# Query and key projections split at group ends, last output tile in halves, written orders replaced

## The chip, the cores and the metric

The kernel runs on one core of a Trainium2 chip. The metric is the device time of one execution in microseconds (us). Five engines work side by side: TensorE (PE in the profile; PEld is its weight load), VectorE (DVE), ScalarE (ACT), GpSimd (POOL) and SyncE (SP), whose queue issues nearly all DMAs here. Each takes its instructions in the order in which the program has them, and waits at an instruction until the semaphores it names have been raised.

## The reference

Two layers follow each other. The first is attention within chunks of 64 tokens, for 8 batches and 8 heads of 64 columns; its output, the heads side by side, is `x` (576 tokens by 512 columns per batch). The second sends `x` through four experts with causal attention over all 576 tokens, and adds the two best experts of each token with softmax weights:

```python
scores = scale * np.matmul(q_c, k_c.transpose(0, 1, 2, 4, 3))      # chunks of 64
attn = softmax(scores); out = np.matmul(attn, v_c)                 # -> x
logits = x @ w_gate; topk = argpartition(-logits, 2); w = softmax(selected logits)
for e in range(E):
    q = x @ wq[e]; k = x @ wk[e]; v = x @ wv[e]
    a = softmax(causal(scale * (q @ k.transpose(0, 2, 1))))
    ye = a @ v @ wo[e]
    out += (weight of e, where e is among the two best) * ye
```

## The kernel before

**Tiles and stages.** The 8 batches of 576 tokens are 36 groups of 128 tokens, nine to every two batches, so a batch is four and a half groups. In an even batch the groups start at columns 0, 128, 256, 384 and 512, and the last one is shared with the next batch; in an odd batch the shared half fills columns 0 to 64 and groups start at 64, 192, 320 and 448. The first five groups are worked one by one, the others mostly in pairs (`UNITS`).

`stage_a` does the first layer of a unit: scores on PE (L471, small 64x64 matmuls on quarters of the array, in two banks of PSUM), row maximum and subtraction on DVE (L481, L483), `exp` on ACT (L486), sum and reciprocal on DVE (L488, L490), the product with the reciprocal on POOL (`en`, L499), a transposition, and the product with the values on PE (L544, quarters again), which ACT and DVE split into a high part `xh` (L557) and a low part `xl` (L559). The first five groups are transposed on PE (L369, then ACT L508); the later ones by a copy on POOL (L376), a transposing DMA and a copy on ACT (L385).

`project_qk` (L588) makes queries (m = 0, 1) and keys (m = 2, 3) of a pair of experts, for a batch in two halves of 288 columns. One half is 12 matmuls of 288 columns into one bank: four slices of the contraction, times three products of high and low parts. ACT then takes the high part out of the bank (L596) and DVE the low part (L601, L604). `project_v` (L443) does the same for the values and the gate, 12 matmuls of 260 columns for 128 tokens.

`scores` (L685) runs on two row halves of the array for two experts at a time, with DVE's masked minimum (L696) and ACT's `exp` (L708) behind it. `weights` multiplies by the gate on POOL (L730) and transposes a head's matrix by PE (L369: 14 small matmuls into two banks, which ACT empties with six copies, L750 and L754), by DVE (L762) and, for the last block of rows, by DMA. `values` (L779) multiplies by the values, `project_out` (L807) by `wo`: 6 matmuls of 512 columns for 128 tokens, one copy of 512 columns out of the bank (DVE for an even tile, L815, ACT for an odd one, L812), one store (L818).

**What sets the order.** `Plan.add` collects every piece of work with its engine, its inputs and the buffers that it needs. `Plan.emit` plays them through with a duration for each and writes the instructions; a buffer (one of 8 banks, for one) goes to whoever asks when it is free in that play. The order on PE, DVE, ACT, POOL and SP is written out in the table `ORDER`: each entry is the number of a piece among those of its engine, and an engine takes nothing but the next one of its list. `CHANGE` holds what the play charges when PE goes from one way of using the array to another: `full` (projections, output), `quarters` (L471, L544), `rows` (L685, L369), `cols` (L779). In the first 25 us of the play, where PE has nothing ready, `emit` puts in a filling matmul (L841, bf16, 512 columns of zeros into a free bank); their number is fixed in the program.

The lines on which the change rests are these:

```python
c0 = 288 * half
...
o = add("PE", 1.595, f, deps=x_done(b, c0, c0 + 288) + [w_op["wqk"][m]], uses=[bk, xs, z])
```

`x_done` gives the pieces that have filled any of these columns of `x`.

Of the kernel before, what the change touches and what calls it, by code (L numbers as in the profile page):

```python
# [36 lines left out]
def rows(i):  # L37
# [4 lines left out]
CHANGE = {("full", "quarters"): 0.138, ("full", "rows"): 0.115, ("full", "cols"): 0.15, ("quarters", "rows"): 0.133, ("quarters", "full"): 0.208,  # L42
          ("quarters", "cols"): 0.164, ("rows", "full"): 0.228, ("rows", "quarters"): 0.161, ("rows", "cols"): 0.184,
          ("cols", "full"): 0.185, ("cols", "quarters"): 0.141, ("cols", "rows"): 0.109}
# [134 lines left out]
def dve_t(n):  # L179
    return 0.075 + 1.04e-3 * n  # L180
# [22 lines left out]
    """,  # L203
    "DVE": """
# [20 lines left out]
    """,  # L225
    "ACT": """
# [55 lines left out]
def chunked_attention_then_attention_experts(ctx: ExitStack, tc: tile.TileContext, qt, kt, vt, wqk, wvg, wo, out):  # L282
# [289 lines left out]
    def project_qk(b, m):  # L572
# [6 lines left out]
        for half in range(2):  # L579
# [15 lines left out]
            def f(bk=bk, cs=cs):  # L595
                act.activation(z.t[hi][:, cs], bk.t[:, :288], AF.Copy, scale=-0.125 if m < 2 else 1.0)  # L596
# [284 lines left out]
```

## Time and profile before

| | |
|---|---|
| median of 3 runs | 382.74 us (382.62 to 382.85) |
| the profiled execution: its time | 382.36 us |
| its span, from the first to the last instruction | 380.4 us |
| PE busy / ACT / DVE / POOL | 372.2 (98%) / 302.6 / 268.5 / 245.1 us |
| granted TensorE clock, mean over the span | 1.000 |
| DMA traffic | 57.24 MB, mean 150 GB/s |

1.96 us of the profiled execution lie outside the span. Matmuls are pipelined: a row gives 0.28 us or so to a matmul whose successor starts 0.12 us later, so PE's 98% is no measure of its throughput, and in what follows the distance between the starts of successive matmuls is used. "Idle before" is time in which an engine ran nothing, with what ended it.

### The profile page before, as it was taken

Reading aid. Unit: us, or ns where it says so; the run is one execution under the profiler, and the core shown is the slowest. Engines: PE = TensorE matmul, PEld = TensorE weight load, DVE = VectorE, ACT = ScalarE, POOL = GpSimd, SP = SyncE. Lnnn points to the kernel's source line nnn. Section 1 sums busy time; section 2 is a strip of 40 time slices with the busy share of each in tenths; the row PEclk is TensorE's granted clock in tenths of the full one; section 3 lists DMA queues with packets and bytes.
Section 4 is the critical chain, followed back from the end, with each engine's and each line's share of the span. In section 5 each row is a group of like instructions: output and inputs, shape, how many; then the busy total and the mean of one; then the engine's idle time right before and its main releaser. Section 6 shows DMA issues by size and latency. Waiting matters only on the chain.

```text
span 380.4 us, 13426 instructions
## 1 busy us (share of the span) xinstructions
PE 372.2 (98%) x5213; PEld 315.7 (83%) x5215; DVE 268.5 (71%) x895; ACT 302.6 (80%) x844; POOL 245.1 (64%) x447
## 2 busy tenths in 40 slices
PE   8999999999999999999999999998999999999996
PEld 3598999977888899788779999877898899977664
DVE  3668878589898775668978487597994298467442
ACT  3555699999958998799887579988996579899731
POOL 7552678986885469975864448959387048876600
PEclk9999999999999999999999999999999999999999
DMA  8977785527779493276989473446786101236534
GB/s 269 392 258 236 201 177 169 98 71 146 130 228 246 93 221 83 57 134 91 293 220 271 137 180 72 112 65 214 142 197 87 25 30 30 30 57 84 165 140 165
DMA packets 88479, 57.24 MB, mean 150 GB/s; under 512 B 68960, under 2 KB 68960, under 8 KB 88416
## 3 DMA queue, kind: packets, MB, share of 16 engines
q1 hardware_dynamic: 88272, 56.12, 59.7%
q8 instruction: 41, 0.67, 0.7%
q10 hardware_dynamic: 144, 0.26, 0.3%
q14 instruction: 22, 0.18, 0.2%
HBM read 30.42 MB, written 9.44 MB: 105 GB/s over the span
## 4 chain that ended last, share of the span: by engine, by line
PE 80%; ACT 9%; DVE 3%; POOL 2%; issue 2%; DMA 2%; POOLq 0%; ACTq 0%; DVEq 0%
PE bank L588 22%; PE bank L443 12%; PE bank L807 12%; PE bank L779 9%; PE bank L685 9%; PE bank L544 4%; PE bank L471 4%; PE bank L369 4%; PE bank L841 3%; ACT at L708 3%; DMA wpT<-wp 2%; POOL at L730 1%; ACT aT L754 1%; ACT aT L385 1%; DVE at L696 1%
## 5 line engine op out<-in xcount | busy, mean ns | idle before, releaser
L730 POOL TENSOR_SCALAR at<-at,st,gate 128x448 f32<-128x448 f32 (+4 forms) x160 | 94.9, 607 | 25.1 <-DVE st L721 21.8
L708 ACT ACTIVATE at<-at,st 64x64 f32<-64x64 f32 (+4 forms) x160 | 88.8, 565 | 4.3 <-DVE st L696 4.1
L588 PE MATMUL bank<-xh,wqk_hi 128*128 128x288 f32 x256 | 77.3, 302 | 0.1
L588 PE MATMUL bank<-xl,wqk_hi 128*128 128x288 f32 x256 | 75.4, 295 | 0.0
L588 PE MATMUL bank<-xh,wqk_lo 128*128 128x288 f32 x256 | 75.4, 294 | 0.0
L696 DVE CUSTOM_DVE_ANT_0 at<-bank,mask 128x448 f32<-128x448 f32 (+4 forms) x160 | 59.9, 421 | 8.0 <-PE bank L685 5.7
L499 POOL TENSOR_TENSOR en<-e,mx 128x512 f32<-128x512 f32 x36 | 37.6, 1058 | 38.3 <-DVE mx L490 23.0
L588 PEld LDWEIGHTS bank<-xh,wqk_hi 128*128 128x128 f32 x256 | 48.0, 187 | 2.5 <-issue 1.0
L588 PEld LDWEIGHTS bank<-xl,wqk_hi 128*128 128x128 f32 x256 | 48.0, 188 | 0.5 <-issue 0.3
L588 PEld LDWEIGHTS bank<-xh,wqk_lo 128*128 128x128 f32 x256 | 48.0, 188 | 0.0
L779 PE MATMUL bank<-aT,vv 128*64 128x448 f32 (+4 forms) x384 | 47.0, 393 | 0.4 <-ACT aT L385 0.3
L779 PEld LDWEIGHTS bank<-aT,vv 128*64 128x64 f32 x384 | 25.0, 137 | 22.3 <-issue 13.7
L385 ACT ACTIVATE aT<-wpT 128x1024 uint16<-128x1024 uint16 x32 | 37.7, 1187 | 3.3 <-DMA wpT<-wp 3.2
L754 ACT ACTIVATE aT<-bank 128x128 f32<-128x128 f32 (+1 forms) x160 | 37.2, 331 | 3.3 <-PE bank L369 2.9
L385 ACT ACTIVATE et<-wpT 128x1024 uint16<-128x1024 uint16 x31 | 36.5, 1183 | 3.6 <-DMA wpT<-wp 3.4
L762 DVE STREAM_TRANSPOSE aT<-at 32x96 f32<-32x96 f32 x128 | 34.4, 269 | 5.3 <-PE bank L779 2.4
L443 PE MATMUL bank<-wvg_hi,xh 128*128 128x260 f32 x128 | 37.0, 289 | 0.0
L376 POOL COPY wp<-at 128x1024 uint16<-128x1024 uint16 x32 | 32.5, 1033 | 6.3 <-DMA wpT<-wp 6.1
L443 PE MATMUL bank<-wvg_lo,xh 128*128 128x260 f32 x128 | 36.3, 283 | 0.0
L443 PE MATMUL bank<-wvg_hi,xl 128*128 128x260 f32 x128 | 36.0, 281 | 0.0
L685 PE MATMUL bank<-kh,qh 64*128 64x288 f32 (+4 forms) x192 | 32.3, 326 | 0.6 <-ACT qh L596 0.5
L376 POOL COPY wp<-en 128x1024 uint16<-128x1024 uint16 x31 | 31.6, 1039 | 1.4 <-DMA wpT<-wp 1.1
(104 smaller groups left out, 895.6 us busy)
## 6 DMA issues: line engine op xcount, KB each, us to landing
ks<-in_kt_dram SPq DMA_DIRECT2D x36, 256.0 KB, 4.4
vs<-in_vt_dram SPq DMA_DIRECT2D x36, 256.0 KB, 4.4
out_dram<-y SPq DMA_DIRECT2D x36, 256.0 KB, 2.1
qs<-in_qt_dram SPq DMA_DIRECT2D x35, 256.0 KB, 4.7
at<-in_wqk_dram SPq DMA_DIRECT2D x4, 256.0 KB, 5.5
wpT<-wp SPq DMA_TRANSPOSE x63, 3.8
at<-in_wvg_dram SPq DMA_DIRECT2D x2, 260.0 KB, 5.6
at<-in_wo_dram SPq DMA_DIRECT2D x2, 256.0 KB, 5.9
```

What stands on the lines that cost most here:

```text
L376: pool.tensor_copy(p.t[:, :256 * n].rearrange("p (x n) -> p x n", x=2), src().bitcast(U16).rearrange("p (n x) -> p x n", x=2))
L385: act.activation(put().bitcast(U16).rearrange("p j (q x) -> p j q x", x=2), pt.t[:, :256 * n].rearrange("p (x j q) -> p j q x", x=2, j=n), ...
L443: pe.matmul(bk.t[0:rows, :W_VG], xp[:, k, cols], wp[:, k, :], start=(n == 0), stop=(n == 3 * KT - 1))
L499: pool.tensor_tensor(en.t.rearrange("p (s h k) -> p s h k", s=2, h=HP), ev, rv.to_broadcast([128, 2, HP, 64]), op=OP.mult)
L588: pe.matmul(bk.t[:, :288], wp[:, k], xp[:, k, c0:c0 + 288], start=(n == 0), stop=(n == 3 * KT - 1))
L685: pe.matmul(bks[s].t[:rows(i), at:at + c1 - c0], q[own, cs], k[own, c0:c1], start=(x == 0), stop=(x == 2), skip_group_check=True)
L696: dve.tensor_tensor_reduce(out=a.t[:r, A_OFF[i] + c0:A_OFF[i] + c1], in0=bk.t[:r, at:at + w], in1=mask[:r, m0:m0 + w], scale=1.0, scalar=f ...
L708: act.activation(af, af, AF.Exp, scale=-1.0, bias=st.t[:r, 0, i, 0:1], accum_out=st.t[:r, 1, i, 0:1])
L730: pool.tensor_scalar(af, af, st.t[:r, 2, i, 0:1], gt.t[:r, i, e:e + 1], op0=OP.mult, op1=OP.mult)
L754: act.activation(dst, bk.t[:, s0:s0 + 64 * n].rearrange("p (j c) -> p j c", j=n), AF.Copy)
L779: pe.matmul(bk.t[64 * s:64 * s + 64, c0 - h0:h1 - h0], vs.t[:, j, 64 * (2 * pair + s):64 * (2 * pair + s) + 64], ts[s].t[:, 448 * j + c0:4 ...
L807: pe.matmul(bk.t, up[:, k, 128 * t:128 * t + 128], wp[:, k, :], start=(n == 0), stop=(n == 5))
```

## The change

There are four edits.

- `project_qk` splits a batch's 576 columns at 256 (even batches) or 320 (odd batches) instead of 288. The first half of an even batch then lies within two groups and the second within the other three; the halves of an odd batch lie within the cut group with the next two, and within the last two. Number and order of matmuls in a half stay, 12; they have 256 or 320 columns.
- `scores` looks up which halves it needs by their new ends.
- The last output tile of the last batch (`b` = 7, `t` = 8) is made in two halves of 256 columns in one bank, 6 matmuls of 256 columns each; DVE copies the first half, ACT the second, and each half has a store of its own.
- Every charge in `CHANGE` is 0.02 higher, and all five lists of `ORDER` are new.

```diff
-CHANGE = {("full", "quarters"): 0.138, ("full", "rows"): 0.115, ("full", "cols"): 0.15, ("quarters", "rows"): 0.133, ("quarters", "full"): 0.208,
+CHANGE = {("full", "quarters"): 0.158, ("full", "rows"): 0.135, ("full", "cols"): 0.170, ("quarters", "rows"): 0.153, ("quarters", "full"): 0.228,
...
     "PE": """
-0 3 6 4 5 1 9 7 2 8 12 58 59 55 57 16 53 10 13 63 11 14 18 54 62 56 64 20 67 68 61 60 17 15 75 76 66 65 89 85 19 87
+3 0 9 4 1 6 2 5 57 61 12 10 7 55 63 53 13 8 11 16 14 58 64 18 60 62 59 73 15 75 76 20 74 56 54 17 68 66 67 65 90 24
...
-            c0 = 288 * half
-
-            def f(bk=bk, c0=c0):
+            c0, c1 = ((0, 256), (256, S))[half] if b % 2 == 0 else ((0, 320), (320, S))[half]
+            n1 = c1 - c0
...
-                        pe.matmul(bk.t[:, :288], wp[:, k], xp[:, k, c0:c0 + 288],
+                        pe.matmul(bk.t[:, :c1 - c0], wp[:, k], xp[:, k, c0:c1],
...
-            o = add("PE", 1.595, f, deps=x_done(b, c0, c0 + 288) + [w_op["wqk"][m]], uses=[bk, xs, z])
+            o = add("PE", 1.595 / 288 * n1, f, deps=x_done(b, c0, c1) + [w_op["wqk"][m]], uses=[bk, xs, z])
...
+            halves = ((0, 256), (256, 512)) if (b, t) == (B - 1, 8) else ((0, 512),)
+            for n0, n1 in halves:
...
+                            pe.matmul(bk.t[:, n0:n1], up[:, k, 128 * t:128 * t + 128], wp[:, k, n0:n1], start=(n == 0),
+                                      stop=(n == 5), skip_group_check=True)
...
+                if t % 2 or n0:
+                    o = add("ACT", act_t(n1 - n0), lambda bk=bk, y=y, n0=n0, n1=n1: act.activation(
+                        y.t[:, n0:n1], bk.t[:, n0:n1], AF.Copy), deps=[o], uses=[bk, y])
+                else:
+                    o = add("DVE", dve_t(n1 - n0), lambda bk=bk, y=y, n0=n0, n1=n1: dve.tensor_copy(
+                        y.t[:, n0:n1], bk.t[:, n0:n1]), deps=[o], uses=[bk, y])
...
+                    nc.sync.dma_start(out[r0:r0 + 128, n0:n1], y.t[:, n0:n1])
```

What moves is seen at three places. Names are those of the code; a number behind a name is the buffer (banks are 61 to 68, `mx_91` is the first group's maximum that is taken), and lines from L589 on stand one to six lines later in the changed kernel.

**First place, the start.** POOL of the kernel before, from its first work on weights:

```order
L419 TENSOR_TENSOR wqk_lo<-at_107,wqk_hi 128x512
L419 TENSOR_TENSOR wvg_lo<-at_108,wvg_hi 128x520
L499 TENSOR_TENSOR en_83<-e_81,mx_91 128x512
L499 TENSOR_TENSOR en_84<-e_82,mx_92 128x512
L419 TENSOR_TENSOR wvg_lo<-at_108,wvg_hi 128x520
L499 TENSOR_TENSOR en_84<-e_81,mx_93 128x512
```

and of the changed kernel:

```order
L419 TENSOR_TENSOR wvg_lo<-at_107,wvg_hi 128x520
L499 TENSOR_TENSOR en_83<-e_81,mx_91 128x512
L499 TENSOR_TENSOR en_84<-e_82,mx_92 128x512
L419 TENSOR_TENSOR wvg_lo<-at_107,wvg_hi 128x520
L419 TENSOR_TENSOR wqk_lo<-at_108,wqk_hi 128x512
L499 TENSOR_TENSOR en_83<-e_81,mx_93 128x512
```

The low part of the first piece of `wqk` was ahead of the first two groups' products and is now behind them.

PE at the start, kernel before, from the last filling matmul to the first query or key projection ("..." stands for rows of the same piece of work):

```order
L841 MATMUL bank_66<-warm 128x512
L544 MATMUL bank_64<-et_87,vs_78 64x64 x2
...
L471 MATMUL bank_67<-ks_73,qs_69 64x64 x2
...
L443 MATMUL bank_66<-wvg_hi,xh_95 128x260
...
L443 MATMUL bank_65<-wvg_hi,xh_95 128x260
...
L588 MATMUL bank_61<-xh_95,wqk_hi 128x288
```

and of the changed kernel:

```order
L544 MATMUL bank_68<-et_85,vs_77 64x64 x2
...
L847 MATMUL bank_66<-warm 128x512
L443 MATMUL bank_62<-wvg_hi,xh_95 128x260
...
L589 MATMUL bank_61<-xh_95,wqk_hi 128x256
...
L471 MATMUL bank_64<-ks_73,qs_69 64x64 x2
```

The first projections stood behind five groups' scores and three groups' value products; now they stand behind four groups' scores and two groups' value products, and the query projection reads the first 256 columns alone. The filling matmuls ahead of them are 47 in the program before and 43 in the changed one.

**Second place, PE near the end**, at the transposition of the last batch's first two heads (L369; `at_109` and `at_110` in the changed kernel, `at_110` and `at_107` before). Kernel before, the first row of each piece, with what it waits for:

```order
L369 MATMUL bank_65<-ident,at_110 128x64 [waits DVE_49,Pool_49]
...
L807 MATMUL bank_64<-wo_hi,uh 128x512 [waits DVE_49]
...
L369 MATMUL bank_67<-ident,at_107 128x64 [waits DVE_49,Pool_49]
...
L807 MATMUL bank_61<-wo_hi,uh 128x512 [waits Activation_49]
```

and the changed kernel:

```order
L369 MATMUL bank_67<-ident,at_109 128x64 [waits DVE_49]
...
L369 MATMUL bank_61<-ident,at_110 128x64 [waits DVE_49]
...
L810 MATMUL bank_67<-wo_hi,uh 128x512 [waits Activation_49]
...
L810 MATMUL bank_62<-wo_hi,uh 128x512 [waits Activation_49]
...
L810 MATMUL bank_66<-wo_hi,uh 128x512 [waits Activation_49]
```

Before, an output tile stood between the two transpositions, and the bank that the next tile took over had been filled a tile earlier. Now the two transpositions follow each other (banks 62 and 67, then 61 and 66), and three output tiles take over three of these four banks at once.

**Third place, the end.** The last rows of DVE and then of ACT in the changed kernel, with what they wait for (a row of before has one copy of 512 columns):

```order
L819 COPY y_125<-bank_61 128x512 [waits DMAHW0_49,PE_49]
L819 COPY y_125<-bank_64 128x256 [waits DMAHW3_49,DVE_49,PE_49]
...
L816 ACTIVATE y_124<-bank_63 128x512 [waits DMAHW2_49,DVE_49,PE_49]
L816 ACTIVATE y_125<-bank_64 128x256 [waits DMAHW3_49,DVE_49]
```

The copy of the second half, on ACT, waits for DVE and not for PE: it has been put behind DVE's copy of the first half, which in turn waits for PE's count after all 12 matmuls of the tile.

## Rows read from the trace of the kernel before

**Rows 1.** The page's head: span, busy time of each engine

```profile
span 380.4 us, 13426 instructions
PE 372.2 (98%) x5213; PEld 315.7 (83%) x5215; DVE 268.5 (71%) x895; ACT 302.6 (80%) x844; POOL 245.1 (64%) x447
```

**Rows 2.** The page's chain that ended last, by engine

```profile
PE 80%; ACT 9%; DVE 3%; POOL 2%; issue 2%; DMA 2%; POOLq 0%; ACTq 0%; DVEq 0%
```

**Rows 3.** Timeline of PE, first 21 us: start, duration, line, work, count

```profile
1.24 4.87 PE L841 MATMUL bank<-warm 128*128 128x512 bf16 x11 [1.24 <-DVE warm L319]
6.05 0.69 PE L471 MATMUL bank<-ks,qs 64*64 64x64 f32 x32
...
8.17 4.05 PE L841 MATMUL bank<-warm 128*128 128x512 bf16 x18 [0.16 <-issue]
...
18.34 0.69 PE L544 MATMUL bank<-et,vs 64*64 64x64 f32 x32
...
20.59 0.39 PE L443 MATMUL bank<-wvg_hi,xh 128*128 128x260 f32 x1
```

**Rows 4.** Timelines of DVE, ACT and POOL in the first 18 us

```profile
6.78 0.76 DVE L481 TENSOR_REDUCE mx<-bank 128x4 f32<-128x256 f32 x2 [5.59 <-PE bank L471]
...
10.42 1.31 POOL L499 TENSOR_TENSOR en<-e,mx 128x512 f32<-128x512 f32 x1 [0.54 <-DVE mx L490]
12.01 1.04 POOL L499 TENSOR_TENSOR en<-e,mx 128x512 f32<-128x512 f32 x1 [0.28 <-DVE mx L490]
...
16.70 0.66 ACT L557 ACTIVATE xh<-bank 128x256 fp32r<-128x256 f32 x2 [1.10 <-PE bank L544]
17.12 0.76 DVE L559 TENSOR_TENSOR xl<-bank,xh 128x256 fp32r<-128x256 f32 x2 [1.10 <-ACT xh L557]
```

**Rows 5.** Timeline of PE, 135 to 146 us: starts of matmuls of three widths

```profile
137.01 0.39 PE L443 MATMUL bank<-wvg_hi,xh 128*128 128x260 f32 x1
137.23 0.28 PE L443 MATMUL bank<-wvg_hi,xl 128*128 128x260 f32 x1
...
139.99 0.29 PE L588 MATMUL bank<-xh,wqk_hi 128*128 128x288 f32 x1
...
143.17 0.28 PE L443 MATMUL bank<-wvg_hi,xh 128*128 128x260 f32 x1
...
144.60 0.39 PE L807 MATMUL bank<-wo_hi,uh 128*128 128x512 f32 x1
...
145.99 0.30 PE L588 MATMUL bank<-xh,wqk_hi 128*128 128x288 f32 x1
```

**Rows 6.** Waits of PE over the whole span: us in total, times, longest

```profile
PE bank L544 <- issue: 1.3, 1, 1.3
...
PE bank L471 <- issue: 0.6, 1, 0.6
PE bank L685 <- ACT qh L596: 0.5, 1, 0.5
```

**Rows 7.** Timeline of ACT at 260 us: six copies that empty a head's two banks

```profile
260.70 0.29 ACT L754 ACTIVATE aT<-bank 128x128 f32<-128x128 f32 x1
260.88 0.28 ACT L750 ACTIVATE aT<-bank 128x128 f32<-128x128 f32 x1
261.04 0.90 ACT L754 ACTIVATE aT<-bank 128x192 f32<-128x192 f32 x4
```

**Rows 8.** Timelines at the end: PE, ACT, SP; copies of 256 columns; the page's stores

```profile
376.40 0.39 PE L807 MATMUL bank<-wo_lo,uh 128*128 128x512 f32 x1
376.82 0.60 ACT L812 ACTIVATE y<-bank 128x512 f32<-128x512 f32 x1 [0.80 <-PE bank L807]
...
19.34 0.42 ACT L557 ACTIVATE xh<-bank 128x256 fp32r<-128x256 f32 x1
19.80 0.42 DVE L559 TENSOR_TENSOR xl<-bank,xh 128x256 fp32r<-128x256 f32 x1 [0.60 <-ACT xh L557]
...
out_dram<-y SPq DMA_DIRECT2D x36, 256.0 KB, 2.1
```

More of the change, by code (lines that the diff above doesn't have):

```diff
@@ L41 @@
 TICK = 3.4133
-CHANGE = {("full", "quarters"): 0.138, ("full", "rows"): 0.115, ("full", "cols"): 0.15, ("quarters", "rows"): 0.133, ("quarters", "full"): 0.208,
-          ("quarters", "cols"): 0.164, ("rows", "full"): 0.228, ("rows", "quarters"): 0.161, ("rows", "cols"): 0.184,
-          ("cols", "full"): 0.185, ("cols", "quarters"): 0.141, ("cols", "rows"): 0.109}
+CHANGE = {("full", "quarters"): 0.158, ("full", "rows"): 0.135, ("full", "cols"): 0.170, ("quarters", "rows"): 0.153, ("quarters", "full"): 0.228,
+          ("quarters", "cols"): 0.184, ("rows", "full"): 0.248, ("rows", "quarters"): 0.181, ("rows", "cols"): 0.204,
+          ("cols", "full"): 0.205, ("cols", "quarters"): 0.161, ("cols", "rows"): 0.129}
 START = {"PE": 0.9, "Pool": 6.0, "ACT": 2.5, "SP": 0.4}
@@ L580, in project_qk, with f @@
             bk = Slot(banks)
-            c0 = 288 * half
-            def f(bk=bk, c0=c0):
+            c0, c1 = ((0, 256), (256, S))[half] if b % 2 == 0 else ((0, 320), (320, S))[half]
+            n1 = c1 - c0
+            def f(bk=bk, c0=c0, c1=c1):
                 w = [t[:, 512 * m:512 * m + 512].rearrange("p (k c) -> p k c", k=KT) for t in W["wqk"]]
@@ L587, in f @@
                     for wp, xp in passes(w, xs.t):
-                        pe.matmul(bk.t[:, :288], wp[:, k], xp[:, k, c0:c0 + 288],
+                        pe.matmul(bk.t[:, :c1 - c0], wp[:, k], xp[:, k, c0:c1],
                                   start=(n == 0), stop=(n == 3 * KT - 1))
                         n += 1
-            o = add("PE", 1.595, f, deps=x_done(b, c0, c0 + 288) + [w_op["wqk"][m]], uses=[bk, xs, z])
-            cs = slice(c0, c0 + 288)
+            o = add("PE", 1.595 / 288 * n1, f, deps=x_done(b, c0, c1) + [w_op["wqk"][m]], uses=[bk, xs, z])
+            cs = slice(c0, c1)
             hi, lo = (0, 1) if m < 2 else (2, 3)
-            def f(bk=bk, cs=cs):
-                act.activation(z.t[hi][:, cs], bk.t[:, :288], AF.Copy, scale=-0.125 if m < 2 else 1.0)
-            o1 = add("ACT", act_t(288), f, deps=[o], uses=[bk, z])
-            def f(bk=bk, cs=cs):
+            def f(bk=bk, cs=cs, n1=n1):
+                act.activation(z.t[hi][:, cs], bk.t[:, :n1], AF.Copy, scale=-0.125 if m < 2 else 1.0)
+            o1 = add("ACT", act_t(n1), f, deps=[o], uses=[bk, z])
+            def f(bk=bk, cs=cs, n1=n1):
                 if m < 2:
-                    dve.scalar_tensor_tensor(z.t[lo][:, cs], bk.t[:, :288], -0.125, z.t[hi][:, cs].bitcast(F32),
+                    dve.scalar_tensor_tensor(z.t[lo][:, cs], bk.t[:, :n1], -0.125, z.t[hi][:, cs].bitcast(F32),
                                              op0=OP.mult, op1=OP.subtract)
                 else:
-                    dve.tensor_tensor(z.t[lo][:, cs], bk.t[:, :288], z.t[hi][:, cs].bitcast(F32), op=OP.subtract)
-            zo.append((hi, c0, add("DVE", dve_t(288), f, deps=[o1], uses=[bk, z])))
+                    dve.tensor_tensor(z.t[lo][:, cs], bk.t[:, :n1], z.t[hi][:, cs].bitcast(F32), op=OP.subtract)
+            zo.append((hi, c0, c1, add("DVE", dve_t(n1), f, deps=[o1], uses=[bk, z])))
     g_op = {}
@@ L672, in scores @@
             for i, c0, c1 in step:
-                need += [o for hi, z0, o in z_op[b, pair] if z0 < (q0(i) + rows(i) if hi == 0 else c1)
-                         and (hi or q0(i) < z0 + 288) and o not in need]
+                need += [o for hi, z0, z1, o in z_op[b, pair] if z0 < (q0(i) + rows(i) if hi == 0 else c1)
+                         and (hi or q0(i) < z1) and o not in need]
                 dur += 0.02 + 3 * max(0.475e-3 * (c1 - c0), 0.11 if i else 0.055)
@@ L800, in project_out @@
             bk, y = Slot(banks), Slot(y_p)
-            def f(t=t, bk=bk):
-                w = [t_.rearrange("p (k c) -> p k c", k=2) for t_ in W["wo"]]
-                n = 0
-                for k in range(2):
-                    for up, wp in ((uh, w[0]), (ul, w[0]), (uh, w[1])):
-                        pe.matmul(bk.t, up[:, k, 128 * t:128 * t + 128], wp[:, k, :], start=(n == 0), stop=(n == 5))
-                        n += 1
-            o = add("PE", 1.41, f, deps=u_op[b] + (u_op[b - 1] if t == 4 else []) + w_op["wo"], uses=[bk])
@@ L810, in project_out @@
-            y_op[b].append(o)
-            if t % 2:
-                o = add("ACT", act_t(512), lambda bk=bk, y=y: act.activation(y.t, bk.t, AF.Copy), deps=[o],
-                        uses=[bk, y])
-            else:
-                o = add("DVE", dve_t(512), lambda bk=bk, y=y: dve.tensor_copy(y.t, bk.t), deps=[o], uses=[bk, y])
-            def f(t=t, y=y):
-                nc.sync.dma_start(out[bb * 2 * S + 128 * t:bb * 2 * S + 128 * t + 128], y.t)
-            o = add("SP", 0.36, f, deps=[o], uses=[y])
@@ L820, in project_out, with f @@
-            transfer("store", 0.6, o, [y])
+            halves = ((0, 256), (256, 512)) if (b, t) == (B - 1, 8) else ((0, 512),)
+            y_op[b].append(None)
+            for n0, n1 in halves:
+                def f(t=t, bk=bk, n0=n0, n1=n1):
+                    w = [t_.rearrange("p (k c) -> p k c", k=2) for t_ in W["wo"]]
+                    n = 0
+                    for k in range(2):
+                        for up, wp in ((uh, w[0]), (ul, w[0]), (uh, w[1])):
+                            pe.matmul(bk.t[:, n0:n1], up[:, k, 128 * t:128 * t + 128], wp[:, k, n0:n1], start=(n == 0),
+                                      stop=(n == 5), skip_group_check=True)
+                            n += 1
+                o = add("PE", 1.41 * (n1 - n0) / 512, f, deps=u_op[b] + (u_op[b - 1] if t == 4 else []) + w_op["wo"], uses=[bk])
+                y_op[b][-1] = o
+                if t % 2 or n0:
[4 more added lines that the diff above has]
+                        y.t[:, n0:n1], bk.t[:, n0:n1]), deps=[o], uses=[bk, y])
+                def f(t=t, y=y, n0=n0, n1=n1):
+                    r0 = bb * 2 * S + 128 * t
+                    nc.sync.dma_start(out[r0:r0 + 128, n0:n1], y.t[:, n0:n1])
+                o = add("SP", 0.36, f, deps=[o], uses=[y])
+                transfer("store", 0.6 * (n1 - n0) / 512, o, [y])
```

136 rows, old and new, of the table ORDER are left out of this document.

## The prediction

> **What bounds the kernel now.** I read the head of the page first: PE is busy 372.2 of 380.4 us, and the next engine, ACT, 302.6 [rows 1]. The chain of work that ended last says the same: 80% of it is PE, 9% ACT [rows 2]. The reader is to see that the time is the sum of PE's own work, and that an edit counts only by what it takes from that work, from the changes between its stages, or from the gaps around it. Then the list of PE's waits: over the whole span only three spells stand in it that matter, 1.3 and 0.6 us whose cause the profile doesn't name ("issue") and 0.5 us for ACT's copy of a query [rows 6]. So PE can gain at the start, where it works on zeros, and at the end, where it is done before the last store; in the middle only little.
>
> The start is read from PE's timeline [rows 3]. PE begins with filling matmuls at 1.24 us, the first real piece is at 6.05, and the first projection at 20.59. Until then the trace has 45 filling matmuls (the program has 47). Eleven of them take 4.87 us, 0.44 each; eighteen later ones 4.05 us, 0.225 each. The filling matmuls are numbers in the program: PE works them off whether or not its data are there.
>
> **Splitting at 256 or 320 columns, by itself.** The work is 384 matmuls of 256 and 384 of 320 columns instead of 768 of 288. The trace has three widths [rows 5]: 260 columns follow each other at (139.99 - 137.23)/23 = 0.120 us, 288 at (143.17 - 139.99)/24 = 0.1325, 512 at (145.99 - 144.60)/6 = 0.232. The line through 260 and 512 puts 256 at 0.118 and 320 at 0.147, together 0.265, as twice 288 does (0.265). So: 0. If 0.120 is already a floor that narrower matmuls don't go below, a pair costs 0.002 more, and with 320 at 0.148 another 0.001: 384 pairs make +1.2 us at most. A gain of more than 0.2 us has no ground in these rows. What the split changes on ACT and DVE (two copies per half, 256 and 320 columns for 288 twice) is as many columns as before in as many copies.
>
> **The start.** The split allows the first half of batch 0 to be projected when two groups are there, not three, and the new lists make use of it: the value projection and a query projection of 256 columns stand behind two groups' value products. Real work that merely moves behind the first projection gains nothing. What gains is filling: 43 in the program for 47, one fewer of the first slow run and three later ones, 0.44 + 3 x 0.225 = 1.1 us. They are spared only if the data are there. The chain of the first two groups [rows 3, 4]: the first scores are done at about 6.3 us, one slow filling matmul earlier than before (6.05 + 0.69 - 0.44); four operations of DVE at 0.38 follow (two take 0.76), to 7.8; the second group's to 9.4; `exp` lies beside them; row sum and reciprocal, some 0.9, to 10.3; POOL's two products 1.31 and 1.04, to 12.6, where a low part of `wqk` no longer stands before them; two transpositions and their copies, to about 13.8; two value products at 0.69, to 15.0; `xh` 0.66 and `xl` 0.76, to 16.4. By the filling matmuls PE comes there at 20.59 - 1.1, less the three pieces (scores, transposition, value product, about 1.6 together) that now stand behind: 17.9. The data are 1.5 us early, so the filling sets the time and 1.1 us is gained: **-1.1**. Bounds: 0, where the loads land as much later as the weights are asked for in another sequence; -2.5, where PE's single short waits between filling runs go too.
>
> **Changes between stages.** Counted in the order, PE changes its way of using the array 108 times instead of 120: from rows to full 18 for 25, from full to rows 16 for 20, the other kinds 74 for 75. One change from rows to full can be seen [rows 5]: the first value matmul is followed after 137.23 - 137.01 = 0.22 us where its successors are followed after 0.12, so a change costs 0.10. Eleven fewer at that price, the others the same: **-1.1**; I take **-1.0**, since full to rows leaves no such row. Bounds: 0 and -1.2. The new charges of `CHANGE` are numbers of the planner's play and no time of the chip.
>
> **Waits in the middle.** Those three waits, 2.4 us [rows 6], belong to the old order, and all pieces have moved. One new wait can be seen in the order, at the second place shown: two heads' transpositions one after the other, then three output tiles that take over three of the four banks. ACT empties a head's two banks with six copies, 260.70 to 261.94, 0.21 each [rows 7]. The first tile needs three of them, 0.65, while PE has only the second transposition (0.5) in between; the second tile needs all six with two of the other head's and an `exp` between them, some 2.5 us, and PE has 0.5 + 1.4. Together about +0.9. Queued behind the waiting matmul is all of PE: the remaining tiles and the last two heads. Elsewhere the order has more room than before: counting pieces at their distances in the trace, a head's last scores stood 19 us of PE's work ahead of its transposition (median) and now 29, a group's value product 11 ahead of its value projection and now 18. I set the new waits at 0.9 seen and 1.0 unseen, against 2.4: **-0.5**. Bounds -2.4 (none) and +2.5 (twice as many as before).
>
> **The last tile in halves.** Before, from the last matmul's start at 376.40: ACT copies 512 columns in 0.60 us from 376.82, and the store lands 2.1 us after its issue [rows 8]. Now the second half's copy waits for DVE's copy of the first half, and that waits for all 12 matmuls, as the third place shows: 0.42 on DVE and then 0.42 on ACT (copies of 256 columns [rows 8]) stand where 0.60 stood, +0.25. Against that, the last store is half as long: at most half of 2.1, but a fixed part stays, I take -0.15. So **+0.1**, bounds -0.8 and +0.3. If the halves were guarded by their own columns, DVE's copy would lie beside the second half's matmuls and ACT's copy would follow at once, 0.42 for 0.60, which with the shorter store makes -0.3.
>
> The Trainium skill, PSUM — Partial Sum Buffer, section "PSUM bank collisions raise a hardware error", says that access to this memory is to be guarded by bank and not by address. By that rule two engines can't share the tile's bank, the halves stand in a row and the sum is the +0.1; without it, the -0.3. No trace of before shows a bank shared in this way.
>
> **The sum.** -1.1 - 1.0 + 0 - 0.5 + 0.1 = -2.5 us, on the profiled execution's 382.36: 379.9. That execution is 0.38 us below the median of the runs, 382.74, so the median of the changed kernel should be 382.74 - 2.5 = **380.2**.
>
> **Rivals.**
> - *The gains are filled by new waits* (no change, 382.7). For it: ACT is 80% busy and every bank goes through its copies; the known waits [rows 6] show up after a single copy that is out of turn. Neighbouring transpositions of two heads have gone from 10 to 12. It needs 2.5 us more of waits than I set, within the bound above. Against: most distances have grown.
> - *ACT's copies come late as a rule* (slower, 385). Place: each of the 12 neighbouring pairs of transpositions, whose four banks the next pieces take over. Price 0.9 apiece [rows 7], as worked out for one of them. PE has room for one such without loss where it has 2.5 us of work on other banks. If six of the twelve lack that room, this is 5.4 us instead of the 0.9 that I counted, +4.5, and 380.2 becomes 384.7. It decides from the fourth on: 380.2 + 3 x 0.9 is 382.9, over 382.74.
> - *The order is better all through* (faster, 377.5). No waits in the middle (-1.9 more) and the start at its better bound (-0.8 more, of 1.4). For it: the longer distances. Against: two of the three known waits [rows 6] have no cause that an order could take away.
> - *The split does nothing*, since odd batches need the same groups for their first half as before and even ones gain one group only. Then the start would still have the fewer filling matmuls, as it is batch 0 that they wait for; the loss is in the distances alone, some 0.5: 380.7. It lies within the forecast.
>
> **How the numbers follow.** The forecast, 378.5 to 381.9, has 0.59. The better order, below 378.5, has 0.13; so faster by over 0.2% (0.77 us, about what a measurement of this kernel can tell from no change), below 381.97, is 0.72. No change within 0.2%, 381.97 to 383.5, has 0.15, and slower 0.13. For the range I add the bounds: all the better ends would give 375 and all the worse ones 386, which don't come together; leaving about 1 in 10 at each side I take 377.3 to 383.2.
>
> **What would show it.** In the timeline of the changed kernel: the first value projection should start near 17.9 us, right behind a run of filling matmuls with no gap; if there is a gap before it, the chain of the data has set the time. Matmuls of 256 columns should follow each other at 0.118 and those of 320 at 0.147; 0.133 or more for 256 would mean a floor and 6 us lost. In PE's waits, an entry for output tiles on ACT's `aT` copies with 0.5 to 0.9 us near the end confirms the second place; several such entries at transpositions confirm the slow rival. At the end, ACT's last copy should start after DVE's last has ended. The forecast falls if PE's waits in the middle come to more than 4 us, or if the first projection is not before 19.5 us.

## The result, and the profile after

The changed kernel takes 378.61 us (median of 4 runs, 377.92 to 378.73) and the kernel before, beside it, 382.68: a ratio of 0.989, interval 0.987 to 0.991. Run again on the chip of the later experiments it took 378.36 us against 382.46, ratio 0.990 (0.986 to 0.993). So it is faster by 4.1 us, or 1.1%; the prediction had 380.2 us, with 377.3 to 383.2 as its range. The profiled execution of the changed kernel took 378.73 us, span 377.0: 3.6 us less than the profiled one of before (382.36, span 380.4).

The head of the page and its chain of work that ended last, to be read beside [rows 1, 2]:

```profile
span 377.0 us, 13434 instructions
...
PE 369.2 (98%) x5214; PEld 315.9 (84%) x5217; DVE 265.9 (71%) x895; ACT 302.5 (80%) x845; POOL 244.9 (65%) x447
...
PE 73%; ACT 10%; DMA 5%; DVE 4%; POOL 4%; issue 2%; SPq 1%; POOLq 0%; ACTq 0%; DVEq 0%
```

PE is still busy for 98% of the span, with 3.0 us less of it, and no other engine has moved by more than 2.6 us. PE's timeline at the start answers to [rows 3]; the row of DVE at its end gives the data that the first projection needs:

```profile
1.24 4.45 PE L847 MATMUL bank<-warm 128*128 128x512 bf16 x10 [1.24 <-DVE warm L319]
5.62 1.13 PE L471 MATMUL bank<-ks,qs 64*64 64x64 f32 x32
...
8.00 0.69 PE L471 MATMUL bank<-ks,qs 64*64 64x64 f32 x32
8.63 3.84 PE L847 MATMUL bank<-warm 128*128 128x512 bf16 x16
...
15.52 1.16 PE L544 MATMUL bank<-et,vs 64*64 64x64 f32 x64
16.84 1.46 PE L847 MATMUL bank<-warm 128*128 128x512 bf16 x6 [0.16 <-issue]
17.95 0.47 PE L443 MATMUL bank<-wvg_hi,xh 128*128 128x260 f32 x1
...
16.69 0.74 DVE L559 TENSOR_TENSOR xl<-bank,xh 128x256 fp32r<-128x256 f32 x2
```

The first projection stands at 17.95 us, right behind a run of filling matmuls, as foretold (17.9). PE's waits over the whole span, beside [rows 6]:

```profile
PE bank L471 <- issue: 1.3, 1, 1.3
...
PE bank L810 <- ACT aT L755: 0.6, 1, 0.6
PE bank L369 <- POOL en L499: 0.3, 1, 0.3
```

The wait for the copy of a query is gone. Of the two without a named cause one is left, at another place (before 221.8 us; in the kernel before they stood before 34.7 and 265.2). The output tiles behind the two neighbouring transpositions wait 0.6 us. The end, from the timelines of PE, DVE and ACT, beside [rows 8]:

```profile
373.22 0.28 PE L810 MATMUL bank<-wo_lo,uh 128*128 128x256 f32 x1
...
373.53 0.42 DVE L819 COPY y<-bank 128x256 f32<-128x256 f32 x1 [3.47 <-PE bank L810]
...
373.99 0.38 ACT L816 ACTIVATE y<-bank 128x256 f32<-128x256 f32 x1 [1.22 <-DVE y L819]
```

ACT's copy starts after DVE's has ended, and the row names DVE as what it waited for.

### The profile page after: what moved, and what is told of

Its sections match the earlier page's. It is cut to its first block, busy times and chain, and to the rows that moved or that the text cites. A ratio compares the mean times of both kernels' runs of the same rounds, so it can differ in the third digit from the quotient of the medians.

```text
span 377.0 us, 13434 instructions
## 1 busy us (share of the span) xinstructions
PE 369.2 (98%) x5214; PEld 315.9 (84%) x5217; DVE 265.9 (71%) x895; ACT 302.5 (80%) x845; POOL 244.9 (65%) x447
## 4 chain that ended last, share of the span: by engine, by line
PE 73%; ACT 10%; DMA 5%; DVE 4%; POOL 4%; issue 2%; SPq 1%; POOLq 0%; ACTq 0%; DVEq 0%
PE bank L589 19%; PE bank L810 14%; PE bank L443 11%; PE bank L780 11%; PE bank L686 8%; ACT at L709 5%; PE bank L544 4%; PE bank L369 4%; PE bank L471 3%; DMA wpT<-wp 2%; DMA vs<-in_vt_dram 1%; POOL at L731 1%; ACT et L385 1%; DMA qs<-in_qt_dram 1%; ACT e L486 1%
## 5 line engine op out<-in xcount | busy, mean ns | idle before, releaser
L731 POOL TENSOR_SCALAR at<-at,st,gate 128x192 f32<-128x192 f32 (+4 forms) x160 | 94.8, 604 | 12.2 <-DVE st L722 4.5
L709 ACT ACTIVATE at<-at,st 128x576 f32<-128x576 f32 (+4 forms) x160 | 89.7, 584 | 4.0 <-DVE st L697 3.8
L589 PE MATMUL bank<-xh,wqk_hi 128*128 128x256 f32 (+1 forms) x256 | 77.3, 302 | 0.0
L589 PE MATMUL bank<-xl,wqk_hi 128*128 128x256 f32 (+1 forms) x256 | 75.7, 296 | 0.0
L589 PE MATMUL bank<-xh,wqk_lo 128*128 128x256 f32 (+1 forms) x256 | 75.7, 296 | 0.0
L697 DVE CUSTOM_DVE_ANT_0 at<-bank,mask 128x320 f32<-128x320 f32 (+4 forms) x160 | 59.9, 421 | 13.7 <-PE bank L686 11.7
L589 PEld LDWEIGHTS bank<-xh,wqk_hi 128*128 128x128 f32 x256 | 48.4, 189 | 2.3 <-issue 0.5
L589 PEld LDWEIGHTS bank<-xl,wqk_hi 128*128 128x128 f32 x256 | 48.5, 189 | 0.2
L589 PEld LDWEIGHTS bank<-xh,wqk_lo 128*128 128x128 f32 x256 | 48.5, 189 | 0.0
L709 ACT ACTIVATION_READ_ACCUMULATOR at<-at,st 128x1 f32 (+1 forms) x160 | 35.4, 221 | 0.0
```

The source lines that it names most:

```text
L589: pe.matmul(bk.t[:, :c1 - c0], wp[:, k], xp[:, k, c0:c1], start=(n == 0), stop=(n == 3 * KT - 1))
L697: dve.tensor_tensor_reduce(out=a.t[:r, A_OFF[i] + c0:A_OFF[i] + c1], in0=bk.t[:r, at:at + w], in1=mask[:r, m0:m0 + w], scale=1.0, scalar=f ...
L709: act.activation(af, af, AF.Exp, scale=-1.0, bias=st.t[:r, 0, i, 0:1], accum_out=st.t[:r, 1, i, 0:1])
L731: pool.tensor_scalar(af, af, st.t[:r, 2, i, 0:1], gt.t[:r, i, e:e + 1], op0=OP.mult, op1=OP.mult)
```

## The experiments

Ratios are to the kernel before, run beside it on the same chip; the number of executions stands in brackets. Profiled executions of one kernel differ by up to 0.7 us at the start alone (the first 32 matmuls took 1.13 us in the rows above and 0.69 in others), so the medians decide and the traces say where.

**1. The split alone**: the kernel before with its own lists, and the projections split at 256 or 320.

```
-            c0 = 288 * half
...
+            c0, c1 = ((0, 256), (256, S))[half] if b % 2 == 0 else ((0, 320), (320, S))[half]
...
```

> The kernel before with its own lists and charges; only the columns are split at 256 or 320. Theory of the prediction: the split by itself is worth nothing (384 pairs of 0.118 and 0.147 us for 0.1325 twice), and the order can't use the looser conditions, so 382.7 within 0.4 us of the kernel before. Rival, the split itself brings the gain (pieces start as soon as their groups are there, even in the old order): 379 to 381. Rival, narrower matmuls have a floor: 384 us or more, with 256 columns at 0.13 us or more. In the trace the waits named issue should stand where they stood before (33.8 and 263.7 us), since the program's instructions are as many.

Measured: 382.93 us (12) against 382.32; ratio 1.003 (1.001 to 1.006). By itself the split is worth nothing, rather 0.3% the other way (0.6 us, where 0.4 was the most expected), so the matmul columns and copies are no source of the gain. The wait of 1.3 us without a named cause stands where it stood (PE stops at 264.1 us); the one of 0.6 us, expected at 33.8 us, doesn't show. What the split does is to allow the new lists, which put a half of 256 columns ahead of the third group's value product. The new lists with the old split were not tried.

**2 and 3. The last tile**: whole again, and its halves with a bank and an output buffer each.

```
-            halves = ((0, 256), (256, 512)) if (b, t) == (B - 1, 8) else ((0, 512),)
+            halves = ((0, 512),)
...
```

> The changed kernel with its last output tile in one piece again: 512 columns, one copy on DVE, one store; all else as in the changed kernel. Theory: the two halves stand one behind the other (DVE 0.42 us, then ACT 0.38), where one copy of 512 columns takes 0.69 on DVE, and the last store is shorter by 0.3 us; together nothing, 378.6 within 0.3 us. Rival, the halves overlap as the edit is written: 0.4 to 0.6 us slower, 379.1.

```
             for n0, n1 in halves:
+                if n0:
+                    bk, y = Slot(banks), Slot(y_p)
```

> The changed kernel, but the two halves of the last tile have a bank and an output buffer each. Theory: ACT's copy of the second half then no longer waits for DVE's copy of the first, and DVE's starts behind the first six matmuls; the last copy ends 0.4 us earlier, so 378.2, 0.3 to 0.5 us faster than the changed kernel. Rival, the two stores at the end set the time: both have to leave through one queue, at 0.4 us an issue, and nothing changes: 378.6.

Measured: whole 378.19 us (6), ratio 0.989 (0.987 to 0.992); two banks 377.66 (6), ratio 0.987 (0.985 to 0.990). The intervals overlap; the traces are sharper. From the end of PE's last matmul to the end of the span it is 380.4 - 376.79 = 3.6 us before and 3.6 whole (372.17 to 375.8), 3.5 with the halves in one bank (373.50 to 377.0) and 3.05 with two (375.15 to 378.2). The timelines of PE, DVE and ACT at the end of the two-bank kernel:

```profile
374.87 0.28 PE L813 MATMUL bank<-wo_lo,uh 128*128 128x256 f32 x1
...
374.50 0.42 DVE L822 COPY y<-bank 128x256 f32<-128x256 f32 x1 [2.79 <-PE bank L813]
...
375.23 0.39 ACT L819 ACTIVATE y<-bank 128x256 f32<-128x256 f32 x1 [0.81 <-PE bank L813]
```

DVE's copy now lies beside the second half's matmuls, and ACT waits for PE. In one bank the two copies stand in a row and nearly all that halving could give is lost. The run gave each half an output buffer of its own as well. PE doesn't touch that buffer, so DVE's earlier copy is due to the bank; for ACT's wait on DVE the run doesn't tell the bank from the buffer.

**4. A tile between the two transpositions**, as in the kernel before: one pair of numbers of PE's list changed places, ACT's list stayed.

```
-301 274 275 297 296 243 213 245 211 298 299 305 304 244 279 276 277 306 307 278 308 310 311 309 312 313
+301 274 275 297 243 296 213 245 211 298 299 305 304 244 279 276 277 306 307 278 308 310 311 309 312 313
```

> The changed kernel with one change in PE's list: near the end, the output tile that waited 0.6 us for ACT's copies now stands between the two heads' transpositions, as one did in the kernel before. Theory: the wait comes from the taken-over bank alone and goes, so 378.0, 0.5 to 0.7 us faster, with no wait of an output tile on aT in the list of PE's waits. Rival, the heads' matrices or the copies on ACT are what is late there: the wait moves to the second transposition or to the value product behind it, and the time stays 378.6.

Measured: 380.36 us (12), ratio 0.995 (0.993 to 0.997): 1.8 to 2.0 us slower than the changed kernel by the medians, which were taken on different chips. Neither expectation came true: the time neither fell nor stayed. The wait has grown from 0.6 to 1.8 us; that is 1.2 us of the difference, and two stretches at a lower clock (last section) add to it in the profiled execution. ACT's timeline, and the tile that waits on PE:

```profile
349.35 0.28 ACT L755 ACTIVATE aT<-bank 128x128 f32<-128x128 f32 x1 [1.27 <-PE bank L369]
349.52 0.66 ACT L709 ACTIVATE at<-at,st 128x448 f32<-128x448 f32 x1
...
350.17 0.27 ACT L755 ACTIVATE aT<-bank 128x128 f32<-128x128 f32 x1
...
350.49 0.73 ACT L755 ACTIVATE aT<-bank 128x192 f32<-128x192 f32 x3
...
351.05 0.50 PE L810 MATMUL bank<-wo_hi,uh 128*128 128x512 f32 x1 [1.79 <-ACT aT L755]
```

The tile in between didn't wait; but the second transposition came a tile later, some 1.5 us, ACT stood idle for 1.27 us until it came, and then had a copy, the 0.66 us `exp` of another head and more copies to do before the next tile's bank was free. So the wait isn't the price of the neighbourhood alone. As the rows read, it goes by how many of ACT's instructions, in ACT's own list, stand between the last transposition and the copy that frees the bank: with a new order on PE and ACT's old one it was three times as long. An ACT list made for this PE order was not tried, so this is a reading of the trace and no test.

**5 and 6. Fewer filling matmuls**: four left out of the kernel before (numbers 10 and 29 to 31), and the six right ahead of the first projection left out of the changed one (37 to 42, in place of the others here).

```
-    plan.emit(lambda: banks and pe.matmul(banks[-1], warm[:, 0:128], warm, start=True, stop=True), WARM)
...
+        if banks and len(made) - 1 not in (10, 29, 30, 31):
+            pe.matmul(banks[-1], warm[:, 0:128], warm, start=True, stop=True)
...
```

> The kernel before with four of its filling matmuls left out (the last three ahead of the first real work behind the second group's scores, and one earlier); everything else as it was. The prediction had the start shorter by 1.1 us since four fewer filling matmuls stand there. Theory A (the filling matmuls set the time of the start): each left out takes 0.23 to 0.27 us off the start, first projection at 19.5 in place of 20.59 us, time lower by about 1.0 us. Theory B (the data set it: the scaled inputs of the first group are ready only just ahead of the first projection): first projection within 0.3 us of 20.59, time lower by 0 to 0.3 us.

> The changed kernel with the six filling matmuls right ahead of the first projection left out. In its trace they run from 16.84 to 18.3 us, and DVE wrote the last of the first projection's input at 17.43 us. Theory A (filling sets the time): first projection at 16.6 to 16.9 in place of 17.95 us, time lower by 1.1 to 1.3 us. Theory B (data and filling end within half a microsecond of each other): first projection at 17.5, time lower by 0.4 us at most; it may be higher by some tenths where TensorE, idle for a microsecond, works on at its lower clock.

Measured: the kernel before with four fewer 381.78 us (11) against 382.46, ratio 0.998 (0.996 to 0.999), -0.7 us; its first projection stands at 19.95 us for 20.59. The missing 0.4 is in its trace: the first scores, due 0.44 us earlier, waited 0.41 us for their keys. The changed kernel with six fewer: 377.35 us (5), ratio 0.987 (0.984 to 0.990), 1.0 us below the changed kernel beside it by the medians (the intervals of the two ratios overlap; the trace decides). Its first projection stands at 16.03 us for 17.95 in the changed kernel's trace: 0.75 of this is the start of that execution, since the first `xl` too is done 0.75 earlier, and 1.2 the filling left out. The filling sets the time in both, as theory A has it. PE's timeline and DVE's of the second one:

```profile
14.77 1.29 PE L544 MATMUL bank<-et,vs 64*64 64x64 f32 x64
...
16.03 0.47 PE L443 MATMUL bank<-wvg_hi,xh 128*128 128x260 f32 x1
16.40 0.39 PE L443 MATMUL bank<-wvg_hi,xl 128*128 128x260 f32 x1
...
15.94 0.74 DVE L559 TENSOR_TENSOR xl<-bank,xh 128x256 fp32r<-128x256 f32 x2
```

Now the data end last: the second matmul, the first that reads `xl`, starts at 16.40, 0.09 us after the first of DVE's two operations (15.94 + 0.37). No more can be had at this place.

**7. The count of instructions.** The wait without a named cause puzzled me: in the changed kernel it stands at PE's record number 7103 (matmuls, weight loads and the few semaphore instructions of their queue, counted from the start; single records are missing from some traces, so a number can be a few off), in the kernel before at 1215 and 8127. Each leaves 191 when divided by 256. PE's instructions come over a queue of their own, the page says, in 41 packets for some 10,520 records, so about 256 each:

```profile
q8 instruction: 41, 0.67, 0.7%
```

So I shifted the count, with the same columns of filling work in more instructions:

```
...
+        w = 128 if 10 <= len(made) < 27 else 512
+        for c in range(0, 512, w) if banks else ():
+            pe.matmul(banks[-1][:, c:c + w], warm[:, 0:128], warm[:, c:c + w], start=True, stop=True)
...
```

> The changed kernel with 17 of the filling matmuls of the start (512 columns) cut into four of 128 columns each: the same columns, and 102 more records of matmuls and weight loads ahead of all real work. The long wait with nothing released (1.3 us at 220.2 us) stands at record 7103 of TensorE in this kernel, at 1215 and 8127 in the kernel before: in each the remainder by 256 is 191. Theory C (the wait belongs to the count of instructions, whose blocks of 256 come over a queue of their own, and shows only where 256 instructions go by in under 3.5 to 4.5 us): with 102 more records the count falls on dense 64x64 stages at 57, 218 and 299 us, where 256 records took 1.9, 1.9 and 2.0 us in the trace. The wait at 220.2 goes, three come of 1.5 to 2.5 us each at these places, and the time rises by 3 to 6 us to 382 to 385 us. Rival D (the wait belongs to this stage, its data or its banks): wait unchanged at 220.2, time within 0.8 us of the changed kernel's.

> The changed kernel again, on the same chip as the three beside it, as their measure. Expected as in its first runs: 378.6 us, ratio to the kernel before 0.989; the 1.3 us wait at the same record (7103).

Measured: 381.39 us (12), ratio 0.996 (0.994 to 0.998), 3.0 us above the changed kernel beside it (378.36, 6 executions). PE's waits of the shifted kernel, and its timeline at 56 and at 219 us:

```profile
PE bank L544 <- issue: 1.3, 1, 1.3
...
PE bank L471 <- issue: 0.7, 1, 0.7
...
55.90 1.11 PE L544 MATMUL bank<-et,vs 64*64 64x64 f32 x63
58.26 0.27 PE L544 MATMUL bank<-et,vs 64*64 64x64 f32 x1 [1.25 <-issue]
...
219.14 0.63 PE L471 MATMUL bank<-ks,qs 64*64 64x64 f32 x28
220.49 0.82 PE L471 MATMUL bank<-ks,qs 64*64 64x64 f32 x36 [0.71 <-issue]
```

A wait has come up at 57 us, where none was, before record 2241, and the one at 220 now stands some 100 records earlier in the work, at record 7105 (both leave 193): the same numbers of the count within two records, in other pieces of work. Rival D has fallen. Of the three waits of 1.5 to 2.5 us that I had forecast two came, of 1.3 and 0.7. The third place, 299 us, showed none, although 256 records passed there in 2.0 us; its packet had set out at 298.67 us, before the dense stage began (299.04), and ended at 299.65, 1.4 us before the next boundary. When a packet is asked for stays open. The two waits are 0.9 us more than the 1.1 of the changed kernel's repetition, so this trace doesn't account for the 3.0 us between the medians: the profiled execution is one of the two shortest (379.21); the other ten, at 380.3 to 383.3, must lose more, and have no trace.

**8. Both gains, and one step more**: six fewer and two banks; and four more filling matmuls left out (23 to 26).

> The changed kernel without the six filling matmuls ahead of the first projection, and with the halves of the last output tile in a bank and an output buffer each. Alone the first gave 1.0 us (377.35 against 378.36 us beside it); the second took the time from the last matmul to the end of the span from 3.8 to 3.3 us in its trace. If the two add up, as they should at opposite ends of the span: 376.9 us, ratio to before 0.986. If one bank more is missing elsewhere (rival): no better than 377.4 us.

> The kernel beside it with four more of the filling matmuls left out, among the 17 between the second and the third group's scores (7.9 to 11.6 us). If filling sets the time there too, 0.9 us more: 376.0 us. If the third group's keys, or the gating's weights, set it: 0 to 0.3 us, and TensorE may work a while at its lower clock, which would make it 0.5 us longer instead. The last is taken as a little likelier, since ScalarE waits for a load (the gating's weights) at 10.8 us in the trace with six fewer.

Measured: 376.80 us (6) against 382.90, ratio 0.985 (0.983 to 0.988), as forecast and the lowest median of this study, 1.6 us below the changed one's on another chip (the intervals of the ratios overlap); and 377.56 (5), ratio 0.986 (0.984 to 0.989). The step more brought nothing, and neither of the reasons that I had given is why. PE's timeline of the last kernel:

```profile
10.97 0.70 PE L471 MATMUL bank<-ks,qs 64*64 64x64 f32 x32
...
14.24 0.92 PE L544 MATMUL bank<-et,vs 64*64 64x64 f32 x45
16.14 0.56 PE L544 MATMUL bank<-et,vs 64*64 64x64 f32 x19 [0.98 <-issue]
```

The third group's scores come at 10.97 for 12.06 us, a gain of 1.1; then PE waits 1.0 us for nothing named, before record 447, which again leaves 191. Its first projection starts at 16.68 us, for 16.38 in the kernel with four more filling matmuls: the wait took back what the start had given. The 0.8 us between the two medians is within their intervals.

## Why the prediction was right, and where it was not

The terms against the two profiled executions, each in us (the sum of the right column is the difference of the profiled times; the medians differ by 0.4 more, since the profiled execution of before lies 0.3 below its median and the changed kernel's 0.1 above):

| term | predicted | measured |
|---|---|---|
| columns of the split | 0 | 0 |
| the start | -1.1 | -1.0 |
| changes between stages | -1.0 | -0.8 |
| waits in the middle | -0.5 | -1.5 |
| the last tile | +0.1 | -0.1 |
| outside the span | 0 | -0.2 |
| sum | -2.5 | -3.6 |

Changes and waits are known best together: from the start of the first projection to the end of the last matmul it is 356.20 us before and 355.55 now, with 1.64 us of moved work in it, so 2.3 less. How these divide rests on usual times and is an estimate. The time outside the span fell from 1.96 to 1.73 us; the prediction had no term for it, and no run shows why.

What the gain hangs on is shown in the main by leaving out: the split alone brings nothing (run 1), the kernel with its last tile whole is as fast (run 2), so it comes with the new lists. The higher charges were not run by themselves, nor the changes between stages. The gain was forecast at 2.5 us and came as 4.1, at the better edge of the forecast's 378.5 to 381.9.

**Columns.** Matmuls of 256 columns follow each other at (20.88 - 19.57)/11 = 0.119 us and those of 320 at (225.54 - 223.93)/11 = 0.146; together 0.265, as before [rows 5]. PE's timeline of the changed kernel, the first and the last of a row of each:

```profile
19.57 0.28 PE L589 MATMUL bank<-xh,wqk_hi 128*128 128x256 f32 x1
...
20.88 0.28 PE L589 MATMUL bank<-xh,wqk_lo 128*128 128x256 f32 x1
...
223.93 0.31 PE L589 MATMUL bank<-xh,wqk_hi 128*128 128x320 f32 x1
...
225.54 0.31 PE L589 MATMUL bank<-xh,wqk_lo 128*128 128x320 f32 x1
```

There is no floor at 260 columns in these rows. That the split brings nothing by itself, as the first run shows, is this term; the 0.6 us by which that run was slower the rows don't explain.

**The start.** From 20.59 to 17.95 us is 2.64, of which 1.64 is work that merely moved behind; the prediction said 1.1 after 1.6. Over five profiled executions with this start the first projection stands between 17.46 and 18.16 us, so the 1.0 is good to half a microsecond. The step "the data are 1.5 us early" was too generous: DVE's first `xl` is done at 17.06 (16.69 + 0.37) and the first matmul that needs it starts at 18.25, so 1.2, and DVE began the second group's work at 8.77 us where the prediction had 7.8, as PE's scores for it came at 8.00. But the conclusion, that the filling sets the time, is shown by runs 5 and 6.

**Changes between stages.** Twelve fewer changes gave 0.76 us, by the time from each piece's first matmul to the next piece's: 0.06 apiece over all kinds, where I had priced eleven at 0.10 and the rest at nothing. Four of the twelve lie ahead of the first projection, which the term of the start covers too.

**Waits in the middle** is the term that was mis-sized. Each piece taken against the usual time of its kind, PE lost 8.1 us after the first projection before and 6.4 now, 1.7 less; the two ends above, 356.20 and 355.55, leave 1.5. The three old waits [rows 6] with what they cost around them were 3.3 us of this; the two of 1.3 and 0.6 us now are 2.4. That is 0.9 less. The remaining 0.6 to 0.8 is spread over many places of less than 0.6 each; I could lay it to none of them, and part may be the error of the usual times. The prediction erred on the other side of the account: it set 1.0 for unseen new waits, and no such sum came. The 0.9 seen in the order came as 0.6, so the step of the two transpositions was right in place and a little high; that undoing this neighbourhood makes it worse (run 4) points to ACT's list, and not to the banks alone. And the waits without a cause were counted as the old order's; run 7 shows that they hang on the count of PE's instructions, and in these traces those of 0.6 us or more come up only in stages of short matmuls. Of two before, one remains, by where the dense stages happen to stand in the new lists. That part of the term was luck: the prediction didn't know what these waits hang on, and the same place costs 0.3 to 1.6 us in one execution or another (last section).

**The last tile.** From the end of the last matmul to that of ACT's copy it is 0.87 us (373.50 to 374.37) for 0.63 before [rows 8], the +0.25 of the prediction; from there to the end 2.63 for 2.98, so the shorter store gave 0.35 where I took 0.15. The Trainium skill, PSUM — Partial Sum Buffer, section "PSUM bank collisions raise a hardware error", asks for guards by bank and not by address. The rows show the program guarded in this way: in one bank DVE's copy waits for the matmuls into the other half's columns, and in two banks it doesn't. What the chip does without such a guard no run here shows.

**The rivals.** The slow one (ACT late at six of twelve neighbouring transpositions) shows once, with 0.6 us; run 4 reads as the same mechanism at 1.8, by one pair of numbers. The rival of the better order all through (377.5) was nearer to the result than the forecast: its waits did shrink, though not to none.

## What to carry to other kernels

Where an engine works on filling ahead of its first real work, leave some of it out in a run by itself: it tells in one look whether filling or data sets the time, and here it was worth as much as the start of the whole change. When an order is edited by hand, the engine that empties the banks needs its list edited too: one pair of numbers on one engine cost nearly 2 us. A wait for "issue" inside a stage of very short instructions should be looked up by its number in the instruction count before the order is blamed for it.

## What the runs showed of the hardware

**Instructions come in blocks, and PE can outrun them.** In the traces of all these kernels, every wait of PE of 0.6 us or more named "issue" stands at a record whose number leaves 190 to 194 by 256: in the kernel before (0.6 and 1.3 us), the changed one (1.3), its repetition (1.1), the shifted one (1.3 and 0.7) and the last (1.0 twice, at 447 and at 7102), and in the others. PE's timeline of the kernel before, then of the changed one:

```profile
34.65 0.34 PE L471 MATMUL bank<-ks,qs 64*64 64x64 f32 x6 [0.61 <-issue]
...
265.19 0.38 PE L544 MATMUL bank<-et,vs 64*64 64x64 f32 x9 [1.31 <-issue]
...
220.11 0.33 PE L471 MATMUL bank<-ks,qs 64*64 64x64 f32 x2
221.76 0.69 PE L471 MATMUL bank<-ks,qs 64*64 64x64 f32 x30 [1.33 <-issue]
```

A packet of instructions had set out shortly before: in the changed kernel its packet ran from 219.38 to 220.33 us, PE stopped after a matmul at 220.21 and went on at 221.76. In every one of these waits PE went on 1.2 to 1.5 us after its packet had ended, and so one place costs more in one execution than in another. At the number 7103 to 7105 the wait was 0.3 us in the whole-tile kernel, whose packet ended at 218.99 us (PE went on at 220.41), and 1.6 in the two-bank one (220.39, and 221.88). The 0.6 us of the kernel before is 0.3 or nothing in runs 1 and 5, whose packets ended 0.9 and 1.1 us ahead of the boundary, for 0.6. All the waits of 0.6 us or more stand in stages of 64x64 matmuls, 0.02 us apart. The Trainium skill, Runtime: NRT & Kernel Launch, section "Instruction fetch mechanics", has blocks of 256 instructions and calls the cost of a boundary mostly hidden. The blocks agree with the count; in these dense stages the cost isn't hidden.

**After such a wait the clock can fall.** In the profiled execution of the two-bank kernel (379.9 us, its median is 377.66) PE waited 1.6 us before 221.9, and then the granted clock was at its lower level, 1.2 GHz, for 3.4 us. The stretches before, in and after it; the columns are length, PE's busy time with its instructions, the granted clock, the DMA engines' share and GB/s:

```profile
215.00:223.30 8.30, 6.71 (x256) 1.00 0.62 191
223.30:226.80 3.50, 3.50 (x17) 0.51 1.43 210
226.80:230.00 3.20, 3.20 (x28) 1.00 0.93 268
```

Matmuls of 320 columns follow each other at 0.267 us in it, for 0.146 in the changed kernel: some 1.6 us lost, on top of the wait. Run 4's profiled execution has two such stretches, one behind each of its waits of 1.6 and 1.8 us; the changed kernel's, after 1.3 us, has none. So a wait of this length can cost twice its own time. It doesn't come in every execution: the mean granted clock is 0.995 in this one and 0.999 to 1.000 in the other five of the two-bank kernel. That the wait is the cause is read from the order of events; no run tests it.
